# Sliding-window attention and a tanh-shrink layer on one core: batch 0's products with V by four query blocks, masks filled by VectorE, the first 760 steps in a new order

## The chip, the cores and the metric

The kernel runs on one core of one Trainium2 chip. A core has five engines that run side by side, each through its own list of instructions, in order: TensorE (PE, matrix products; PEld in the profile is its loading of weights), VectorE (DVE), ScalarE (ACT), GpSimd (POOL) and SyncE (SP). They wait for one another on semaphores. Data come from and go to the chip's memory by DMA transfers, which SP and POOL start here. Products land in PSUM, eight banks of 128 partitions x 2 KB; PE writes them, DVE and ACT read them, POOL does not.

The metric is the device time of one execution in microseconds (us).

## The reference

Eight batches of eight heads with 576 tokens of 64 numbers go through causal attention in a window of 64 tokens. The output, as 4,608 tokens of 512 numbers, goes through two dense layers.

```python
scores = scale * np.matmul(q, k.transpose(0, 1, 3, 2))
mask = (rel >= 0) & (rel < window)        # rel = query position - key position, window = 64
attn = softmax(where(mask, scores, -1e9))
x = matmul(attn, v), heads side by side   # 4608 x 512
h = x @ w_in                              # 512 x 2048
out = (h - np.tanh(h)) @ w_out            # 2048 x 512
```

## The kernel before

**Tiling.** A "group" g is a pair of heads of one batch (four groups to a batch, b = g // 4), and the 576 queries of a group are nine blocks of 64. A block of queries needs 128 keys. The tokens of all batches, put behind one another, are nine "chunks" of 512; a chunk c is worked through both dense layers by 16 tiles m of the hidden dimension and four row tiles s of the output. Since a batch has nine blocks and a chunk eight, the ninth block of batch 0 belongs to chunk 1.

**What sets the order.** Nothing is scheduled by a tool. A string PLAN lists some 2,000 steps, and `play` issues them one by one; each engine gets its instructions in the order in which the steps stand. A step is a short name with numbers, and ends in the engine's letter where it can run on several (p GpSimd, a ScalarE, v VectorE, s SP). A number at the end is often a PSUM bank. The steps that matter here, with the lines of the profile:

- `lk.g`, `lq.g` (L110): load K or Q of a group, 144 KB as stored; `LV.b.i`, `lv.b.pair.half` (L145, L132): load V; `wi.i` (L188), `wo.i` (L198): load parts of w_in (two of 256 columns, then three of 512) and w_out; `qr`, `lr`, `tq`, `tk`: rows of Q and K of batches 3 and later and their transposes by DMA on SP (L166, L171, L179).
- `U.n.bank` (L227): n products on a tile of zeros that nothing reads; fillers.
- `i` (L202), `h` (L230), `n` (L237): make the identity and two masks.
- `ck`, `cq` (L90 on ACT, L92 on DVE): cast or lay out rows for PE; `Fp`, `Ep` (L256, L260): PE's transposes of K and Q; `Fc`, `Ec` (L90, L92): copy them out of PSUM to kt and qp.
- `Rp.g.half.bank` (L281, L286): scores of five or four blocks; in batch 0 a product with the mask `hide` comes first. `Rx` (L318): Exp on ScalarE. `M` (L323): masking on VectorE, batch 1 and later.
- `zr`, `za`, `zb`, `Z`: copies of V between the halves of the partitions.
- `P`, `D`, `DS`, `DH` (L335, L375 to L390): in batch 0, a group's products with V into two banks, and the division by the row sums; `PP`, `DR`, `DN`: the same for two groups in later batches.
- `Xp`, `Xc` (L397): transposes of the attention output and their copies to x of a chunk (xT).
- `Hp.c.m.half`, `H.c.m` (L508, L431): first layer, a half or a whole tile m; `A` (L439): tanh; `G` (L445): the subtraction; `W.c.s.part` (L474): second layer; `O.c.s` (L90, L92 and a store by SP): output.

The products of the first layer of chunk 0 go round three PSUM banks, and of later chunks two; a bank is free when `G` has read it. GpSimd starts at most eight loads ahead: each further one waits until the load eight places before it has landed.

In batch 0, `P` did two banks of five blocks; as there are only nine, the ninth was computed twice:

```python
for n in range(2):
    for i in range(5):
        j = min(5 * n + i, NJ - 1)
```

Of the kernel before, what the change touches and what calls it, by code (L numbers as in the profile page):

```python
# [7 lines left out]
F32 = mybir.dt.float32  # L8
# [7 lines left out]
def kernel(  # L16
# [184 lines left out]
    def make_ident():  # L201
        nc.gpsimd.memset(ident, 0.0)  # L202
# [26 lines left out]
    def make_hide():  # L229
        nc.gpsimd.memset(hide, 0.0)  # L230
# [5 lines left out]
    def make_mask():  # L236
        nc.gpsimd.memset(seen, 1.0)  # L237
# [8 lines left out]
    def chunk_tile(c):  # L246
        return x_chunk[c % 3]
# [77 lines left out]
    def pv_banks(g):  # L325
        return ps[:, 0:2, :] if g == 2 else ps[:, 5:7, :]

    def pv(g):
        b, pr = divmod(g, NP)
        for n in range(2):  # L330
            for i in range(5):
                j = min(5 * n + i, NJ - 1)
                for h in range(2):
                    r = slice(64 * h, 64 * h + 64)
                    nc.tensor.matmul(pv_banks(g)[r, n, 65 * i:65 * i + 65], PT[g % NPT][:, j, r],  # L335
                                     vw[b % 2][:, j, pr + NP * h, :], start=True, stop=True)
# [34 lines left out]
    def norm(g):  # L371
        b, pr = divmod(g, NP)
        ov = pv_banks(g)[:, :, 0:5 * (D + 1)].rearrange("p n (i c) -> p n i c", c=D + 1)
        rc = sm_pool.tile([128, 2, 5, 1], F32, tag="rc", name="rc")
        nc.vector.reciprocal(rc, ov[:, :, :, D:D + 1])  # L375
        xo = xs[b % 2][:, pr // 2].rearrange("p (n i) r d -> p n i r d", i=5)
        nc.vector.tensor_tensor(xo[:, :, :, pr % 2, :], ov[:, :, :, 0:D], rc.to_broadcast([128, 2, 5, D]), ALU.mult)

    last = {}

    def norm_sums(g):
        ov = pv_banks(g)[:, :, 0:5 * (D + 1)].rearrange("p n (i c) -> p n i c", c=D + 1)
        last[g] = sm_pool.tile([128, 2, 5, 1], F32, tag="rc", name="rc")
        nc.vector.reciprocal(last[g], ov[:, :, :, D:D + 1])

    def norm_half(g, n):
        b, pr = divmod(g, NP)
        k = 5 - n
        ov = pv_banks(g)[:, n, 0:k * (D + 1)].rearrange("p (i c) -> p i c", c=D + 1)
        nc.vector.tensor_tensor(xs[b % 2][:, pr // 2, 5 * n:5 * n + k, pr % 2, :], ov[:, :, 0:D],  # L390
# [260 lines left out]
```

## Time and profile before

| | us |
|---|---|
| median of three runs | 307.96 (307.23 to 308.13) |
| span of the profiled execution | 305.2 |
| time around the span, median less span | 2.76 |
| PE busy | 297.8 (98%) |
| VectorE busy | 176.2 (58%) |
| ScalarE busy | 157.5 (52%) |
| GpSimd busy | 103.7 (34%) |

The profile shows one execution, from its first to its last instruction. The profiled execution's own time is known as its span alone, 305.2 us; the runs were timed apart from it. A line of the timeline reads: start in us, length in us, engine, source line, operation, output <- input, partitions x elements, how many were merged, and in brackets how long the engine was idle before and what ended that. A busy PE is not a PE at its peak: products overlap, and one with 512 columns is shown with 0.38 us while the next can start 0.21 us behind it.

### The profile page before, as it was taken

The page shows a single profiled execution, that of the slowest core. Times are in us where ns is not written, and L with a number is a line of the kernel's source. Part 1 is how long each engine was busy: PE and PEld are TensorE (multiplying, and loading weights), DVE is VectorE, ACT ScalarE, POOL GpSimd, SP SyncE. Part 2 cuts the span into 40 slices and gives each one's busy share as a digit, 9 for nine tenths or more (in the row PEclk, how much of TensorE's full clock was granted, in tenths as well). Part 3 has the DMA queues.
Part 4 walks back from the last instruction along what each step waited for, and adds up shares of the span by engine and source line. Part 5 has one row for each costly group of instructions (what it writes and reads, how often), then busy time and mean ns, then how long its engine had stood idle before and what let it go on. Part 6 is the DMA issues. An engine that isn't in the chain of part 4 may idle for free.

```text
span 305.2 us, 6469 instructions
## 1 busy us (share of the span) xinstructions
PE 297.8 (98%) x2599; PEld 149.4 (49%) x2632; DVE 176.2 (58%) x316; ACT 157.5 (52%) x265; POOL 103.7 (34%) x141
## 2 busy tenths in 40 slices
PE   8999999999999999999999999999999999999995
PEld 3574555545455545444544444444544444444443
DVE  1687993289577745675387475657673645355300
ACT  1898975487565346534564645345633433433211
POOL 8989775800994290019005770000000000000000
PEclk9999999999999999999999999999999999999999
DMA  9999999995999999949999999560143010001112
GB/s 155 159 195 193 195 207 180 159 205 102 102 143 127 173 125 181 182 108 131 164 177 127 135 173 142 95 143 35 37 76 74 0 69 37 34 34 37 52 51 104
DMA packets 132878, 36.77 MB, mean 120 GB/s; under 512 B 119920, under 2 KB 127344, under 8 KB 132848
## 3 DMA queue, kind: packets, MB, share of 16 engines
q0 software_dynamic: 92752, 18.06, 85.3%
q1 hardware_dynamic: 40096, 18.30, 31.5%
q8 instruction: 20, 0.33, 0.5%
q14 instruction: 10, 0.08, 0.1%
HBM read 36.70 MB, written 9.44 MB: 151 GB/s over the span
## 4 chain that ended last, share of the span: by engine, by line
PE 87%; DVE 5%; ACT 3%; issue 2%; POOL 2%; DVEq 0%; ACTq 0%; POOLq 0%
PE ps L474 38%; PE ps L431 30%; PE ps L508 6%; PE ps L348 3%; PE ps L304 2%; DVE gT L445 2%; PE ps L397 1%; ACT th L439 1%; PE ps L286 1%; PE ps L467 1%; DVE pt L323 1%; PE ps L260 1%; PE ps L281 1%; PE ps L227 1%; POOL qall L110 1%
## 5 line engine op out<-in xcount | busy, mean ns | idle before, releaser
L445 DVE TENSOR_TENSOR gT<-ps,th 128x512 bf16<-128x512 f32 x144 | 97.2, 687 | 85.3 <-ACT th L439 84.6
L474 PE MATMUL ps<-w_out_sb,gT 128*128 128x512 bf16 x527 | 131.5, 380 | 2.2 <-issue 0.8
L439 ACT ACTIVATE th<-ps 128x512 f32<-128x512 f32 x144 | 84.7, 599 | 93.0 <-PE ps L431 79.7
L431 PE MATMUL ps<-xT,wi 128*128 128x512 bf16 x496 | 120.7, 380 | 0.1
L474 PEld LDWEIGHTS <-gT 128*128 128x128 bf16 x560 | 53.3, 98 | 61.4
L431 PEld LDWEIGHTS <-wi 128*128 128x128 bf16 x496 | 47.0, 98 | 54.3
L145 POOL DMA_DIRECT2D vw<-in_v_dram x35 | 30.0, 872 | 36.1 <-PE ps L348 33.5
L90 ACT ACTIVATE ysb<-ps 128x512 f32<-128x512 f32 (+1 forms) x24 | 14.2, 593 | 30.9 <-PE ps L474 30.2
L166 POOL DMA_DIRECT2D qall<-in_q_dram x25 | 21.7, 881 | 24.1 <-DMA qw<-qall 21.4
L166 POOL DMA_DIRECT2D kall<-in_k_dram x25 | 21.7, 875 | 10.4 <-DMA kw<-kall 4.8
L314 ACT ACTIVATE pt<-ps 128x1024 bf16<-128x1024 f32 (+1 forms) x30 | 23.3, 816 | 3.5 <-PE ps L304 3.2
L323 DVE TENSOR_TENSOR pt<-pt,ps 128x1152 bf16<-128x1152 bf16 x28 | 20.5, 749 | 5.1 <-ACT pt L314 3.2
L508 PE MATMUL ps<-xT,wi 128*128 128x512 bf16 x80 | 20.8, 380 | 0.0
L92 DVE COPY ysb<-ps 128x512 f32<-128x512 f32 (+1 forms) x11 | 7.1, 650 | 20.5 <-PE ps L467 13.2
L368 DVE TENSOR_TENSOR xs<-ps,rcp 128x384 bf16<-128x384 f32 x28 | 15.2, 550 | 0.3
L318 ACT ACTIVATE pt<-ps 128x640 bf16<-128x640 f32 (+1 forms) x24 | 14.7, 659 | 0.8 <-PE ps L286 0.8
L348 PEld LDWEIGHTS <-pt 128*64 128x64 bf16 x504 | 9.4, 112 | 6.3 <-DVE pt L323 2.1
L90 ACT ACTIVATE kt<-ps 128x576 bf16<-128x576 bf16 x10 | 6.5, 647 | 10.8 <-PE ps L256 6.8
L227 PE MATMUL ps<-warm 128*128 128x512 bf16 (+1 forms) x35 | 10.6, 435 | 1.1 <-DVE warm L207 1.1
L508 PEld LDWEIGHTS <-wi 128*128 128x128 bf16 x80 | 7.4, 98 | 8.5 <-issue 0.4
L348 PE MATMUL ps<-vw,pt 128*64 128x65 bf16 x504 | 11.0, 197 | 0.3 <-DVE pt L323 0.2
L365 DVE TENSOR_TENSOR xs<-ps,rcp 128x384 bf16<-128x384 f32 x14 | 7.7, 550 | 0.1
(74 smaller groups left out, 166.7 us busy)
## 6 DMA issues: line engine op xcount, KB each, us to landing
out_dram<-ysb SPq DMA_DIRECT2D x33, 256.0 KB, 3.1
vw<-in_v_dram POOLq DMA_DIRECT2D x28, 128.0 KB, 6.6
qall<-in_q_dram POOLq DMA_DIRECT2D x20, 128.0 KB, 7.5
kall<-in_k_dram POOLq DMA_DIRECT2D x20, 128.0 KB, 6.8
w_out_sb<-in_moe_w_out_dram POOLq DMA_DIRECT2D x4, 512.0 KB, 8.2
kall<-in_k_dram POOLq DMA_DIRECT2D x11, 144.0 KB, 6.3
qall<-in_q_dram POOLq DMA_DIRECT2D x11, 144.0 KB, 6.6
wi<-in_moe_w_in_dram POOLq DMA_DIRECT2D x3, 512.0 KB, 7.9
```

Source lines behind the costliest of these rows:

```text
L90: nc.scalar.activation(o, i, ACT.Copy)
L145: nc.gpsimd.dma_start(out=w[:, 2 * i + 1, :, 0:D] if i < NF else w[64:128, 2 * i, :, 0:D], in_=v[b, :, 128 * i:128 * i + n].rearrange("h p ...
L166: nc.gpsimd.dma_start(out=token_rows(b, n)[0:c, i], in_=(q if n == "q" else k)[b, :, 128 * i:128 * i + c].rearrange("h p d -> p h d"))
L314: nc.scalar.activation(o, sp, ACT.Exp, scale=scale)
L323: nc.vector.tensor_tensor(p, p, mask.unsqueeze(1).to_broadcast([128, 2 * NJ, 64]), ALU.mult)
L348: nc.tensor.matmul(ps[r, bank, 65 * i:65 * i + 65], PT[(g + r2) % NPT][:, j, r], vw[b % 2][:, j, p0 + r2 + NP * h, :], start=True, stop=True)
L368: nc.vector.tensor_tensor(xs[b % 2][:, p0 // 2, 0:6, n // 2, :], ov[:, :, 0:D], sums[g][:, n].to_broadcast([128, 6, D]), ALU.mult)
L431: nc.tensor.matmul(hp, w_in_tile(ki, m), chunk_tile(c)[:, n.start // 64:n.stop // 64, ki % 2, 64 * (ki // 2):64 * (ki // 2) + 64], start=( ...
L439: nc.scalar.activation(th[:, n], hp, ACT.Tanh)
L445: nc.vector.tensor_tensor(gT[c][:, m, columns(s)], hp, th, ALU.subtract)
L474: nc.tensor.matmul(yp, gT[c][:, m, s * 128:(s + 1) * 128], w_out_sb[:, m, :], start=n == 1 and i == 0, stop=n == 4 and i == 3)
L508: nc.tensor.matmul(hp, w_in_tile(half + 2 * i, m), chunk_tile(c)[:, :, half, 64 * i:64 * i + 64], start=n == 1 and i == 0, stop=n == 2 and ...
```

## The change

In batch 0 the products with V of a group (`Pn`, `pv_part`) are made for four query blocks at a time, into one bank each (blocks 0 to 3 or 4 to 7), with their own reciprocals (`Dr`) and normalisation (`Dn`) on VectorE or, once, on ScalarE by four copies with a scale. The ninth blocks of all four groups are done together (`Pe`), normalised (`De`), transposed (`Xe`) and copied (`Xf`) to chunk 1. The transposes of xs in batch 0 then have four blocks in each part. A new step `iv` lets VectorE fill the identity's and the masks' tiles, which GpSimd did. The PLAN's steps up to `DR.22` stand in another order, with 16 fillers in place of 35; behind that step nothing is changed.

```diff
     def make_ident():
-        nc.gpsimd.memset(ident, 0.0)
         nc.gpsimd.affine_select(ident, ident, compare_op=ALU.not_equal, fill=1.0,
                                 base=0, pattern=[[-1, 128]], channel_multiplier=1)
+
+    def fill_masks():
+        nc.vector.memset(ident, 0.0)
+        nc.vector.memset(hide, 0.0)
+        nc.vector.memset(seen, 1.0)
...
-    def pv(g):
+    def pv_part(g, n, bank):
         b, pr = divmod(g, NP)
-        for n in range(2):
-            for i in range(5):
-                j = min(5 * n + i, NJ - 1)
-                for h in range(2):
-                    r = slice(64 * h, 64 * h + 64)
-                    nc.tensor.matmul(pv_banks(g)[r, n, 65 * i:65 * i + 65], PT[g % NPT][:, j, r],
-                                     vw[b % 2][:, j, pr + NP * h, :], start=True, stop=True)
+        for i in range(4):
+            j = 4 * n + i
+            for h in range(2):
+                r = slice(64 * h, 64 * h + 64)
+                nc.tensor.matmul(ps[r, bank, 65 * i:65 * i + 65], PT[g % NPT][:, j, r],
+                                 vw[b % 2][:, j, pr + NP * h, :], start=True, stop=True)
+
+    def pv_ends(b, bank):
+        for pr in range(NP):
+            for h in range(2):
+                r = slice(64 * h, 64 * h + 64)
+                nc.tensor.matmul(ps[r, bank, 65 * pr:65 * pr + 65], PT[(NP * b + pr) % NPT][:, NJ - 1, r],
+                                 vw[b % 2][:, NJ - 1, pr + NP * h, :], start=True, stop=True)
...
+    def norm_part(g, n, bank, eng):
         b, pr = divmod(g, NP)
...
+        if eng is nc.scalar:
+            for i in range(4):
+                nc.scalar.activation(xo[:, i], four(bank)[:, i, 0:D], ACT.Copy, scale=last[g, n][:, i])
+        else:
+            nc.vector.tensor_tensor(xo, four(bank)[:, :, 0:D], last[g, n].to_broadcast([128, 4, D]), ALU.mult)
...
     PLAN = """
-        u mv.0 mv.1 lk.1.p lq.2.p LV.0.2 U.1.3 U.1.3 U.1.5 U.1.7 U.1.6 lk.3.p U.1.1 U.1.7 lk.2.p U.1.7 lq.1.p
...
+        u iv U.8.3 U.4.4 lq.0.s lq.3.p lk.0.s i lk.2.p lk.3.p ck.0.a Fp.0.5 cq.0.a Fc.0.5.a mv.0 mt.0 mk mt.3
```

Three places show what moved. In the rows, kall0 and qall0 are the loaded K and Q of batch 0, kall1 and qall1 those of batch 1, vw0 is V of batch 0, ps the PSUM, pt the probabilities, xs the normalised attention output. The line numbers of the changed kernel are its own.

GpSimd's first transfers and masks, before:

```order
L110 DMA kall0_104<-in_k_dram 96x2x384
L110 DMA qall0_102<-in_q_dram 96x2x384
L145 DMA vw0_85<-in_v_dram 128x8x64
L110 DMA kall0_104<-in_k_dram 96x2x384 x2
L110 DMA qall0_102<-in_q_dram 96x2x384 x2
L145 DMA vw0_85<-in_v_dram 128x8x64
L202 MEMSET ident_75 128x128
L203 ISA
L203 AFFINE_SELECT ident_75<-ident_75 128x128
L145 DMA vw0_85<-in_v_dram 128x8x64 x2
```

and now:

```order
L110 DMA qall0_102<-in_q_dram 96x2x384
L202 ISA
L202 AFFINE_SELECT ident_75<-ident_75 128x128
L110 DMA kall0_104<-in_k_dram 96x2x384 x2
L145 DMA vw0_85<-in_v_dram 128x8x64
L110 DMA qall0_102<-in_q_dram 96x2x384
L110 DMA kall0_104<-in_k_dram 96x2x384
L234 AFFINE_SELECT hide_78<-hide_78 128x128
L236 AFFINE_SELECT hide_78<-hide_78 128x128
L145 DMA vw0_85<-in_v_dram 128x8x64 x3
L110 DMA qall0_102<-in_q_dram 96x2x384
L110 DMA kall1_105<-in_k_dram 96x2x384
```

The identity stands behind the first load in place of the eighth, both steps on `hide` come before the last V tiles, and the last Q of batch 0 (group 2's) is the tenth load, where it was the second.

ScalarE ahead of the copies to xT of chunk 0, before (from the eighth and last Exp of batch 0 to the first tanh):

```order
L318 ACTIVATE pt_87<-ps_74 128x640
L90 ACTIVATE kb2_111<-kall1_105 96x2x6x64
L90 ACTIVATE kt0_88<-ps_74 128x576
L90 ACTIVATE qp0_94<-ps_74 128x576
L90 ACTIVATE qb2_108<-qall1_103 96x2x6x64
L90 ACTIVATE kt1_89<-ps_74 128x576
L318 ACTIVATE pt_87<-ps_74 128x512
L90 ACTIVATE xT0_112<-ps_74 128x4x128
L90 ACTIVATE kb1_110<-kall1_105 96x2x6x64
L439 ACTIVATE th_596<-ps_74 128x512
```

and now, from the copy of group 2's Q on:

```order
L90 ACTIVATE qp2_96<-ps_74 128x576
L320 ACTIVATE pt_87<-ps_74 128x512
L390 ACTIVATE xs0_115<-ps_74,rh_404 128x64 x4
L320 ACTIVATE pt_87<-ps_74 128x640
L320 ACTIVATE pt_87<-ps_74 128x512
L90 ACTIVATE qb1_107<-qall1_103 96x2x6x64
L90 ACTIVATE kt2_90<-ps_74 128x576
L90 ACTIVATE xT0_112<-ps_74 128x4x128
L90 ACTIVATE qb0_106<-qall1_103 96x2x6x64
L90 ACTIVATE xT0_112<-ps_74 128x4x128 x2
```

Two casts of batch 1's Q (qb) stand between the last Exp of batch 0 and the copies to xT, and ScalarE does one normalisation in four parts.

VectorE from the V copies to the first normalisation, before:

```order
L92 COPY vw0_85<-vw0_85 64x520 x6
L92 COPY kb1_110<-kall1_105 96x2x6x64
L375 RECIPROCAL rc_386<-ps_74 128x10
L377 TENSOR_TENSOR xs0_115<-ps_74,rc_386 128x10x64
L92 COPY qb1_107<-qall1_103 96x2x6x64
```

and now:

```order
L92 COPY vw0_85<-vw0_85 64x520 x8
L92 COPY kb0_109<-kall1_105 96x2x6x64
L383 RECIPROCAL rh_400<-ps_74 128x4
L383 RECIPROCAL rh_402<-ps_74 128x4
L383 RECIPROCAL rh_404<-ps_74 128x4
L392 TENSOR_TENSOR xs0_115<-ps_74,rh_402 128x4x64
L392 TENSOR_TENSOR xs0_115<-ps_74,rh_400 128x4x64
```

The cast kb0 (step `ck.6`, K of group 6, the eleventh load) stands ahead of three reciprocals in a row, and each normalisation covers four blocks of one group in place of ten.

More of the change, by code (lines that the diff above doesn't have):

```diff
@@ L379 @@
[L379 to L390, printed above, removed]
-                                last[g][:, n, 0:k].to_broadcast([128, k, D]), ALU.mult)
+    last = {}
@@ new lines, in norm_ends, with x_ends @@
+    def norm_ends(b, bank):
+        rc = sm_pool.tile([128, 4, 1], F32, tag="rh", name="rh")
+        nc.vector.reciprocal(rc, four(bank)[:, :, D:D + 1])
+        for half in range(2):
+            n = slice(2 * half, 2 * half + 2)
+            nc.vector.tensor_tensor(xs[b % 2][:, half, NJ - 1], four(bank)[:, n, 0:D],
+                                    rc[:, n].to_broadcast([128, 2, D]), ALU.mult)
+    def x_ends(b, bank):
+        tp = ps[:, bank, :].bitcast(BF16)[:, 0:256].rearrange("p (r t) -> p r t", t=128)
+        for half in range(2):
+            nc.tensor.transpose(tp[:, half, :], xs[b % 2][:, half, NJ - 1].rearrange("p r d -> p (r d)"), ident)
@@ L400, in x_put @@
     def x_put(b, half, part, bank, eng):
-        w0, w1 = 4 * part, 4 + 5 * part
+        w0, w1 = 4 * part, 4 + (5 if b else 4) * part
         tp = ps[:, bank, :].bitcast(BF16)[:, 0:640].rearrange("p (w t) -> p w t", t=128)
```

190 lines of the change are left out of this document (95 added, 95 removed).

## The prediction

> **What bounds the kernel now.** I read the page's busy times first, then the chain that ended last, then what TensorE (PE) waited for.
>
> ```profile
> PE 297.8 (98%) x2599; PEld 149.4 (49%) x2632; DVE 176.2 (58%) x316; ACT 157.5 (52%) x265; POOL 103.7 (34%) x141
> PE 87%; DVE 5%; ACT 3%; issue 2%; POOL 2%; DVEq 0%; ACTq 0%; POOLq 0%
> PE ps L227 <- DVE warm L207: 1.1, 1, 1.1
> PE ps L474 <- issue: 0.8, 5, 0.2
> ```
>
> PE carries 87% of the chain and hardly waits: its longest wait for another engine is the first 1.1 us. Nothing that only frees ScalarE, VectorE or GpSimd can shorten this kernel. What can go is work of PE that computes nothing: the filler products of line 227.
>
> ```profile
> L227 PE MATMUL ps<-warm 128*128 128x512 bf16 (+1 forms) x35 | 10.6, 435 | 1.1 <-DVE warm L207 1.1
> 1.06 6.54 PE L227 MATMUL ps<-warm 128*128 128x512 bf16 x22 [1.06 <-DVE warm L207]
> 8.33 1.90 PE L227 MATMUL ps<-warm 128*128 128x512 bf16 x7
> 1.47 0.15 PEld L227 LDWEIGHTS <-warm 128*128 128x128 bf16 x1 [0.28 <-issue]
> 1.89 0.15 PEld L227 LDWEIGHTS <-warm 128*128 128x128 bf16 x1 [0.28 <-issue]
> 4.56 2.55 PEld L227 LDWEIGHTS <-warm 128*128 128x128 bf16 x12 [0.28 <-issue]
> 22.58 1.54 PE L508 MATMUL ps<-xT,wi 128*128 128x512 bf16 x6
> ```
>
> Fillers of 512 columns start 0.43 us apart at first (1.47 to 1.89) and about 0.21 apart from 4.56 on (12 in 2.55), so PE runs at half pace for its first 3.5 us. All 35 take about 6.5 + 1.7 + 6 x 0.22 = 9.5 us of PE's time. They cover the time in which the inputs arrive and attention of batch 0 is too short of work; the first product with w_in (step Hp.0.0.0) starts at 22.58. From there PE is dense, as the stages show:
>
> ```profile
> 5.50:22.58 17.08, 16.63 (x324) 10.64 (x323) 10.84 (x30) 13.14 (x22) 15.15 (x26) 1.00 1.70 176
> 22.58:41.12 18.54, 18.52 (x207) 9.48 (x205) 16.01 (x34) 16.48 (x31) 14.17 (x23) 1.00 1.44 196
> 41.12:195.00 153.88, 152.11 (x1402) 77.05 (x1423) 97.92 (x168) 85.41 (x144) 70.06 (x85) 1.00 1.79 149
> ```
>
> (Columns: stretch, its length, busy PE, weight loads, DVE, ACT, POOL, clock, DMA, GB/s.) After 41 us there is nothing to win, only something to lose. So the question is when Hp.0.0.0 starts in the new order, and whether PE stays fed behind it.
>
> **The change part by part.** *Fillers.* 19 of 35 go. Twelve stand at the start: 8 at 0.43 and 4 at 0.21 from 1.06 end at about 5.3; four more (0.86 us) stand before the third group of scores. That is 5.1 us in place of 9.5. The 4.4 us are saved only if PE has real work then; else they become waits.
>
> *Work before and behind Hp.0.0.0.* These rows give prices on PE:
>
> ```profile
> 18.98 0.43 PE L260 MATMUL ps<-ident,kb 96*128 96x96 bf16 x6
> 14.11 0.29 PE L286 MATMUL ps<-qp,kt 64*128 64x64 bf16 x8
> 16.06 0.51 PE L335 MATMUL ps<-vw,pt 128*64 128x65 bf16 x20
> ```
>
> By Hp.0.0.0 the new order has done less: one transposed half of batch 1 in place of four (3 x 0.25, without the 0.17 tail of the last), no Rp.4.1.5 (0.3), 16 fewer products with V (0.35) and 2 fewer transposes of xs (0.1): 1.5 us. Of that 8 products (0.18) are gone for good, the last blocks no longer being done twice, and two later fillers (0.43) go too. So 0.9 us more is left behind Hp.0.0.0, and the change breaks even if that step starts at 22.58 - 0.9 = 21.7.
>
> *When it can start: the loads.*
>
> ```profile
> 1.28 0.43 SPq L110 DMA_DIRECT2D qf<-in_q_dram  x1
> qf<-in_q_dram SPq DMA_DIRECT2D x1, 288.0 KB, 3.7
> 7.53 0.48 PEld L256 LDWEIGHTS <-qall 96*64 96x64 bf16 x12 [0.42 <-DMA qall<-in_q_dram]
> 15.30 0.65 POOL L110 DMA_DIRECT2D qall<-in_q_dram  x1 [0.27 <-DMA vw<-in_v_dram]
> 21.04 0.64 POOL L110 DMA_DIRECT2D qall<-in_q_dram  x1 [0.83 <-DMA wi<-in_moe_w_in_dram]
> ```
>
> SP's second load lands at 1.28 + 3.7 = 5.0; it is K of group 0 now, and ScalarE's cast can begin then, where before it began at 9.11. GpSimd's loads share some 176 GB/s. Before, its second had landed by 7.5, its tenth by 15.3 (GpSimd, eight loads on, waits for it), its seventeenth (10 x 144 + 4 x 128 + 64 + 2 x 256 = 2,528 KB in) by 21.0. In the new order its tenth load is Q of group 2, the last input that batch 0's attention needs; the first ten carry the same 6 x 144 + 4 x 128 KB. I take 14.6, between 13.5 (no queueing behind it) and 15.3.
>
> *When it can start: the engines.* Durations:
>
> ```profile
> 9.11 0.84 ACT L90 ACTIVATE kb<-kf 96x768 bf16<-96x768 f32 x1
> 11.46 0.65 ACT L90 ACTIVATE qp<-ps 128x576 bf16<-128x576 bf16 x1
> 13.37 3.50 ACT L318 ACTIVATE pt<-ps 128x640 bf16<-128x640 f32 x6
> 22.26 0.60 ACT L90 ACTIVATE xT<-ps 128x512 bf16<-128x512 bf16 x1
> 44.88 0.77 ACT L90 ACTIVATE xT<-ps 128x384 bf16<-128x384 bf16 x2 [0.79 <-PE ps L397]
> 15.76 0.36 DVE L92 COPY kb<-kall 96x768 bf16<-96x768 bf16 x1
> 16.68 0.22 DVE L375 RECIPROCAL rc<-ps 128x10 f32<-128x10 f32 x1 [0.56 <-PE ps L335]
> 21.14 0.41 DVE L390 TENSOR_TENSOR xs<-ps,rc 128x256 bf16<-128x256 f32 x1
> ```
>
> Back to back, ScalarE's jobs start about 0.1 sooner than their durations say (six Exp in 3.50). Group 0's scores can begin near 8.7, when the third load has been transposed, four us earlier than before. But PE then outruns the loads: from Q of group 2 at 14.6 on there are its transposes (to 15.0), the copy on ScalarE (15.1 to 15.7) and one Exp (to 16.2). VectorE meanwhile stands in step ck.6, whose K of group 6 is the eleventh load (15.5), and only then does its three reciprocals (0.22 each); behind it stand all normalisations, so the banks of PE too. ScalarE resumes at about 16.9 with the four scaled copies of Dn.3.1.6. No row shows a copy of 128x64: 0.07 each by elements from the 128x384 copies (0.77 for two), 0.39 if as long as one of those; I take 0.2, nearer the small end. Then in its order two Exp, the cast cq.4, a copy, an xT copy, the cast cq.6 and the last xT copy: 0.8 + 1.1 + 0.73 + 0.53 + 0.48 + 0.73 + 0.6 = 5.0. Hp.0.0.0 starts at 21.8 or so; with the ends of both unknowns, 20.4 to 22.9. Against 21.7 that is a loss of 0.1 us. The two casts (1.5 us) belong to batch 1 and stand ahead of a copy on which PE waits.
>
> *The first layer behind it.*
>
> ```profile
> 27.79 2.75 PE L431 MATMUL ps<-xT,wi 128*128 128x512 bf16 x12
> 29.55 1.63 ACT L439 ACTIVATE th<-ps 128x512 f32<-128x512 f32 x3
> ```
>
> PE needs 0.86 us a tile; sixteen tanh at about 0.5, with the casts, copies and Exp between, are about 15 of the 16.5 us that PE takes here, so ScalarE just keeps up. The weights come in the order wi.0, wi.3, wi.1, wi.2, wi.4. wi.3 is complete at 2,928 KB: (2,928 - 2,528) / 196 behind 21.0 is 23.0, likewise wi.1 24.4, wi.2 27.0, wi.4 30.3. Counting its work from Hp.0.0.0 on, PE wants them at about 24.8, 27.4, 28.7 and 32, so each has 1.7 us to spare. The three banks of the first layer are freed tile by tile (tanh, then VectorE's subtraction): I find two waits of 0.2 there, so I charge 0.4 us, between 0 and 1.2.
>
> *Batch 1's products with V, behind the W steps.* They now wait at the end of VectorE's two maskings and two V copies (0.7 each), which start once the Exp of group 7 is done, behind an output copy on ScalarE. I get 51.2 against PE's 50.7: 0.4, ends 0 and 1.
>
> *Masks.* Three fills move from GpSimd to VectorE:
>
> ```profile
> 7.02 0.27 POOL L202 MEMSET ident<- 128x128 bf16 x1
> 8.18 0.76 DVE L92 COPY qp<-ps 128x576 bf16<-128x576 bf16 x1 [5.21 <-PE ps L256]
> ```
>
> They fall into VectorE's 5.2 us of idle time: nothing; were it busy, 0.1 each. On GpSimd they free 0.3 us each, and its loads wait for their turn on the DMA engines anyway. *Casts moved to GpSimd* (ck.4, cq.9, cq.10, ck.11): about 0.9 us each by elements (768 for 520) from the row below. K of group 4 is there near 28 and PE asks for it at 31.6; for cq.10 I get 57.4 against 61. So nothing; if that cover fails, 0.9 each on PE, and the loads queued behind them are as late.
>
> ```profile
> 29.43 0.61 POOL L92 COPY vw<-vw 64x520 bf16<-64x520 bf16 x1
> ```
>
> *Switches between kinds of products on PE*: scores of batch 1 now stand singly in places, two more returns to long products, 0.1 each: 0.2.
>
> The sum: 305.2 + 0.1 + 0.4 + 0.4 + 0.2 = 306.3 us of span. The median of 307.96 is 2.76 more than the profiled span, which I keep: 309.1.
>
> **The rivals.** *Faster: the ladder is shorter.* It decides from Hp.0.0.0 before 20.6, so that 1.1 us is gained and what follows costs nothing. If Q of group 2 lands at 13.5, PE's own chain of scores (to about 14) governs, ck.6 does not wait, and with short scaled copies Hp.0.0.0 starts near 20.4: 307.96 - 1.3 = 306.7. For it speaks that ScalarE works from 5.0, not 8.4; against it the tenth load at 15.3 in the row above.
>
> *Slower: PE falls back to half pace.* From 5.3 to about 8.7 PE has 36 short transposes, some 1.2 us of work in 3.4, where before fillers filled such gaps. If it then runs at half pace until it has been busy as long as at the start, some 5 us of real work up to 16 (six sets of scores at 0.5 with their masks, five transposed halves at 0.3) take twice as long, half of that in waits that are there anyway: +2.5, 311.6. The granted clock reads 1.00 in each stretch, even where the first fillers run at half pace, so it cannot exclude it. [...]
>
> *Slower: a late V copy.*
>
> ```profile
> 75.95 5.94 POOL L145 DMA_DIRECT2D vw<-in_v_dram  x7 [15.41 <-PE ps L348]
> 71.37 24.11 SPq L171 DMA_TRANSPOSE kw<-kall  x3
> vw<-in_v_dram POOLq DMA_DIRECT2D x28, 128.0 KB, 6.6
> ```
>
> GpSimd's queue already stands 15 us behind PE once. In the new order loads of batch 5 (qr.5.1), which need batch 3's transposes on SP done, stand ahead of LV.3.0, which VectorE's Z.3 needs at about 85. Batch 1's last products free V's buffer near 56; some twenty issues at 0.85 (seven in 5.94) and a wait for SP bring GpSimd to LV.3.0 near 76, and it lands 6.6 later, near 83. Four us later still it would hold VectorE for 2, and PE through the banks: +2, 311.
>
> **How the numbers follow.** No change is told from a change of under 0.3%, 0.92 us. The forecast has 0.55 (0.33 of it slower by more, 0.22 within 0.92 us, by the ends of its four terms, 307.5 to 310.5), the short ladder 0.26, half pace 0.07, the late V copy 0.12. So faster 0.26, same 0.22, slower 0.52. The range leaves out 0.1 on each side: 306.5 to 311.4.
>
> **What would show it.** Right: Hp.0.0.0 (first product on xT) between 21 and 22.5; VectorE idle before ck.6's copy until K lands; ScalarE without a gap from 17 to 21.5; PE's waits up to there some 5 us in place of fillers; first-layer tiles done near 39. Wrong: Hp.0.0.0 before 20.6; any product of 512 columns 0.43 apart behind 5.3; a PE wait of over 1 us behind 41.

## The result and the profile after

The changed kernel takes 312.29 us (median of four, 310.68 to 312.74), the kernel before 307.94 on the same chip: a ratio of 1.0137 (95% interval 1.0106 to 1.0168), 4.35 us slower. The forecast had the sign right (309.1, slower with 0.52), but the time lies above its range, which ended at 311.4. The ratios here and below leave out the executions over 1.5% longer than the fastest of the same kernel (four, all with two or four stretches at half pace: two with five output buffers, one with Q of group 2 earlier, one with six fillers); the medians don't.

The page of the changed kernel, its busy times, the clock that PE was granted (in 40 slices of 7.8 us, tenths of full speed) and the chain that ended last:

```profile
PE 299.2 (96%) x2571; PEld 150.0 (48%) x2605; DVE 177.3 (57%) x325; ACT 158.2 (51%) x268; POOL 105.4 (34%) x141
PEclk9957999999999999999999999999999999999999
PE 90%; DMA 4%; POOL 2%; issue 1%; DVE 1%; ACT 1%; POOLq 0%; DVEq 0%; ACTq 0%
```

The third and fourth slices are new: PE runs there at half pace in part. And PE now waits, where before it had one wait of 1.1 us at the start and little else:

```profile
PE ps L526 <- DMA xT<-xs: 1.8, 1, 1.8
PE ps L258 <- DMA qall<-in_q_dram: 1.2, 2, 0.8
PE ps L231 <- DVE warm L211: 1.1, 1, 1.1
PE ps L415 <- DVE xs L392: 1.0, 2, 0.7
PE ps L333 <- ACT pt L320: 0.7, 1, 0.7
```

The stages of the changed kernel, cut where the granted clock changes (columns as in the prediction; the clock is the third number from the end):

```profile
10.08:13.49 3.41, 3.41 (x62) 1.82 (x60) 1.80 (x6) 2.79 (x5) 3.41 (x6) 1.00 1.76 157
13.49:16.90 3.41, 1.90 (x62) 1.40 (x56) 1.22 (x6) 1.97 (x4) 3.15 (x5) 1.00 1.29 172
16.90:20.31 3.41, 3.41 (x54) 2.17 (x53) 2.48 (x11) 2.90 (x8) 2.76 (x6) 0.50 1.40 193
20.31:23.73 3.42, 2.40 (x25) 1.80 (x24) 1.21 (x4) 3.42 (x6) 1.58 (x3) 0.50 1.33 203
23.73:27.14 3.41, 3.41 (x19) 1.71 (x16) 0.70 (x3) 1.85 (x4) 1.50 (x3) 0.50 1.26 205
```

From 16.90 to 27.14 us the clock is 0.50. That is 10.24 us, three stretches of 3.41: in two other profiles (below) the clock stays at 0.50 for 3.41 us, and full pace lasts 10.24 us here ahead of the fall (from 6.66), 283.31 behind it (83 stretches) and 300.37 in the profile before (4.70 to 305.07, 88 stretches). In the stretch ahead of the fall PE was busy for 1.90 of 3.41 us.

The rows of PE on the ladder that the prediction built, and the one late wait:

```profile
14.39 0.45 PE L258 MATMUL ps<-ident,qall 96*64 96x96 bf16 x12 [0.82 <-DMA qall<-in_q_dram]
16.08 0.70 PE L333 MATMUL ps<-vw,pt 128*64 128x65 bf16 x32 [0.69 <-ACT pt L320]
23.57 1.06 PE L526 MATMUL ps<-xT,wi 128*128 128x512 bf16 x2
149.51 0.59 PE L526 MATMUL ps<-xT,wi 128*128 128x512 bf16 x2 [1.84 <-DMA xT<-xs]
```

L526 is the first half product of a chunk, and its first row is Hp.0.0.0: at 23.57, where before it stood at 22.58. The second of its two products starts at 23.99, 0.43 behind the first: half pace. The last row is Hp.4.0.1, which waits for a transpose of xs by DMA (step Y.4.1, L434). SP issued that transpose behind two transposes of K and a store:

```profile
139.31 2.51 SPq L171 DMA_TRANSPOSE kw<-kall  x2
141.91 0.53 SPq L513 DMA_DIRECT2D out_dram<-ysb  x1
142.54 3.06 SPq L434 DMA_TRANSPOSE xT<-xs  x2
```

Before, the same step left 6.4 us earlier (3.8 earlier than in the second profile of the changed kernel, below), and no PE wait of over 0.2 us stood in the second half of the kernel:

```profile
136.13 2.62 SPq L416 DMA_TRANSPOSE xT<-xs  x2
```

ScalarE's four scaled copies, whose price no row of before showed:

```profile
17.23 0.93 ACT L390 ACTIVATE xs<-ps,rh 128x64 bf16<-128x64 f32 x4 [1.20 <-DVE rh L383]
```

So there were two suspects, the half pace and the wait of 1.84 us.

### The profile page after: what moved, and what is told of

The parts are those of the page before. It is cut to its first block, busy times and chain, and to the rows that moved or that the text cites. A ratio compares the mean times of both kernels' runs of the same rounds, so it can differ in the third digit from the quotient of the medians.

```text
span 310.9 us, 6430 instructions
## 1 busy us (share of the span) xinstructions
PE 299.2 (96%) x2571; PEld 150.0 (48%) x2605; DVE 177.3 (57%) x325; ACT 158.2 (51%) x268; POOL 105.4 (34%) x141
## 4 chain that ended last, share of the span: by engine, by line
PE 90%; DMA 4%; POOL 2%; issue 1%; DVE 1%; ACT 1%; POOLq 0%; DVEq 0%; ACTq 0%
PE ps L492 38%; PE ps L449 34%; PE ps L526 6%; PE ps L353 3%; DMA xT<-xs 2%; PE ps L306 2%; DMA qall<-in_q_dram 2%; PE ps L415 2%; PE ps L262 2%; PE ps L288 1%; PE ps L485 1%; POOL vw L145 1%; PE ps L333 1%; POOL kall L110 1%; POOL qall L110 0%
## 5 line engine op out<-in xcount | busy, mean ns | idle before, releaser
L492 PE MATMUL ps<-w_out_sb,gT 128*128 128x512 bf16 x526 | 129.9, 379 | 2.0 <-issue 0.5
L325 DVE TENSOR_TENSOR pt<-pt,ps 128x1152 bf16<-128x1152 bf16 x28 | 20.4, 750 | 8.4 <-ACT pt L316 4.7
L526 PE MATMUL ps<-xT,wi 128*128 128x512 bf16 x80 | 22.4, 398 | 2.0 <-DMA xT<-xs 1.8
L166 POOL DMA_DIRECT2D qall<-in_q_dram x25 | 21.5, 863 | 4.0 <-DMA qw<-qall 2.0
L320 ACT ACTIVATE pt<-ps 128x512 bf16<-128x512 f32 (+1 forms) x24 | 15.0, 652 | 8.2 <-PE ps L288 7.4
L373 DVE TENSOR_TENSOR xs<-ps,rcp 128x384 bf16<-128x384 f32 x28 | 14.8, 550 | 0.2
L92 POOL COPY q<-qw 64x256 bf16<-64x256 bf16 x3 | 1.2, 402 | 34.6 <-DMA qw<-qall 34.6
L526 PEld LDWEIGHTS <-wi 128*128 128x128 bf16 x80 | 7.7, 102 | 9.9 <-issue 2.9
L90 ACT ACTIVATE xT<-ps 128x512 bf16<-128x512 bf16 (+3 forms) x12 | 5.8, 516 | 6.4 <-PE ps L415 6.4
L110 POOL DMA_DIRECT2D qall<-in_q_dram x11 | 7.3, 670 | 3.2 <-DMA w_out_sb<-in_moe_w_out_dram 1.9
```

Source lines behind the costliest of these rows:

```text
L90: nc.scalar.activation(o, i, ACT.Copy)
L166: nc.gpsimd.dma_start(out=token_rows(b, n)[0:c, i], in_=(q if n == "q" else k)[b, :, 128 * i:128 * i + c].rearrange("h p d -> p h d"))
L320: nc.scalar.activation(PT[g % NPT][:, js[0]:js[0] + len(js), :].rearrange("p i (h t) -> p i h t", h=2), sp, ACT.Exp, scale=scale)
L325: nc.vector.tensor_tensor(p, p, mask.unsqueeze(1).to_broadcast([128, 2 * NJ, 64]), ALU.mult)
L492: nc.tensor.matmul(yp, gT[c][:, m, s * 128:(s + 1) * 128], w_out_sb[:, m, :], start=n == 1 and i == 0, stop=n == 4 and i == 3)
L526: nc.tensor.matmul(hp, w_in_tile(half + 2 * i, m), chunk_tile(c)[:, :, half, 64 * i:64 * i + 64], start=n == 1 and i == 0, stop=n == 2 and ...
```

## The experiments

All ran beside the kernel before: the run without its last six fillers on one chip (median of the kernel before 308.06), all others on another, called the second chip below (307.70 to 307.95). A useful measure comes with each execution: its mean granted clock. One stretch of 3.41 us at half pace lowers the mean over some 309 us by 3.41 x 0.5 / 309 = 0.0055, so a clock of 0.994 means one such stretch, 0.989 two and 0.983 three. The values of 0.997 to 0.999 I put down to the very end of a run, behind its last products: in the profile of the new code in the old order (0.998) the last 1.4 us are at half pace, in the first of the changed kernel the last 0.42, and PE does nothing there.

### The changed kernel again

No edit.

> The changed kernel once more, unaltered, on the same chip as the experiments beside it, for its spread and its granted clock from execution to execution. If the fall of the clock is what makes its executions differ, those of clock 1.00 are some 2 us shorter than those near 0.985. Rival (the landing of transfers makes them differ): executions of equal clock differ by as much.

311.11 us (309.12 to 313.47, ten executions), ratio 1.0095 (1.0061 to 1.0129). Three executions had a clock of 0.998 or more: 309.12, 309.66 and 309.94, mean 309.57. The other seven had 0.993 to 0.995, one stretch at half pace each: 310.77 to 313.47, mean 311.81. The first chip's four fit: 310.68 at 1.00, 312.02 and 312.74 at 0.989 and 0.988, 312.57 at 0.983. The kernel before never fell below 0.998 in the 88 executions beside these runs. Over both chips the four executions at full pace have a mean of 309.85, the ten with half pace 312.00, 2.1 us more. Executions of equal clock still differ by up to 2.7 us, so the rival has a part too.

The profiled one had a clock of 1.00 and a span of 308.0. Its waits and its Hp.0.0.0:

```profile
PE ps L258 <- DMA qall<-in_q_dram: 1.4, 2, 0.8
PE ps L526 <- DMA xT<-xs: 1.3, 1, 1.3
PE ps L415 <- DVE xs L392: 1.2, 2, 0.7
PE ps L231 <- DVE warm L211: 1.1, 1, 1.1
PE ps L262 <- ACT kb L90: 0.8, 1, 0.8
PE ps L449 <- DVE gT L463: 0.7, 1, 0.7
PE ps L333 <- ACT pt L320: 0.7, 1, 0.7
...
22.22 0.59 PE L526 MATMUL ps<-xT,wi 128*128 128x512 bf16 x2
```

At full pace Hp.0.0.0 starts at 22.22. With three more waits of 0.3, 0.2 and 0.2 PE waits 6.8 us behind its start, against 0.4 before; 2.0 of the 6.8 (xT and gT) lie behind 41 us.

What the half pace itself costs is seen when the two profiles of this one kernel are laid side by side. ScalarE's scaled copies start at 17.23 in the first, where half pace has just begun (16.90 to 27.14), and here at 17.20; the first Exp behind the half pace starts there at 28.64 and here at 25.55:

```profile
17.20 0.93 ACT L390 ACTIVATE xs<-ps,rh 128x64 bf16<-128x64 f32 x4 [1.20 <-DVE rh L383]
28.64 0.60 ACT L320 ACTIVATE pt<-ps 128x512 bf16<-128x512 f32 x1 [1.19 <-PE ps L288]
25.55 0.60 ACT L320 ACTIVATE pt<-ps 128x512 bf16<-128x512 f32 x1 [0.44 <-ACT th L457]
```

(The middle row is of the first profile, the others of this one.) So the two are level to 0.03 us up to the fall, and the first is 3.1 us late behind three slow stretches, though PE waited no longer in it (1.2 us between 17 and 41, against 1.7 here). At the end it is 2.9 us late, the whole difference of the two spans. In one stretch at half pace PE can lose no more than half of it, 1.7 us. The seven executions with one stretch are 2.2 us longer in the mean than the three without, so the half pace is most of that but, as far as so few can tell, not all: a load that lands late makes PE wait, and the same wait empties a stretch (in the first profile the 0.82 us on Q of group 2 lie in the stretch from 13.49, ahead of the fall).

### The kernel before without 13 fillers

```diff
-Fp.1.5 U.1.2 Ec.2.3.v ... mt.1 U.1.1 U.1.3 U.1.2 U.1.4 mt.2 U.1.1 U.1.4 cq.0.a ... Ep.1.3 U.1.7 Fp.3.5
+Fp.1.5 Ec.2.3.v ... mt.1 mt.2 cq.0.a ... Ep.1.3 Fp.3.5
...
-P.3 U.1.3 lk.6.p ... lq.7.p U.1.4 ... Rp.4.1.5 U.1.1 ... Hp.0.1.0 U.1.5 ... N U.1.7
+P.3 lk.6.p ... lq.7.p ... Rp.4.1.5 ... Hp.0.1.0 ... N
```

> The kernel before without its 13 fillers behind the first 22 (3.2 us of PE's time between 8 and 28 us). Theory of the clock: without them PE has waits there, the granted clock falls under 1.00 somewhere between 12 and 27 us, and the time rises by 1 to 3 us, to 309 to 311. Rival 1 (the fillers cost what they take): 305.0. Rival 2 (waits take their place and the clock stays at 1.00): 307.6 to 308.

308.57 us, ratio 1.0031 (1.0007 to 1.0054). Nine of ten executions had a clock of 0.983 to 0.994, and the time goes with it: 307.82 at 1.00; 308.03 in the mean with one stretch (five), 309.15 with two (three), 310.02 with three (one). The clock fell where the theory said, but the rise in time is below its 1 to 3 us. Neither rival came: some 3 us less work of PE made the kernel slower by 0.8 in the medians (0.2 to 1.7 by the ratio). The stretches of the profile, cut at the same period:

```profile
5.63:9.05 3.42, 3.06 (x35) 1.44 (x33) 0.57 (x1) 0.32 (x1) 3.35 (x6) 1.00 1.54 176
9.05:12.46 3.41, 2.05 (x60) 1.70 (x60) 1.50 (x7) 3.22 (x6) 3.27 (x8) 1.00 2.16 163
12.46:15.87 3.41, 3.16 (x36) 1.34 (x36) 2.66 (x9) 2.51 (x5) 2.86 (x5) 0.50 1.81 153
15.87:19.28 3.41, 3.41 (x54) 1.78 (x52) 0.53 (x3) 2.36 (x4) 2.89 (x5) 0.50 1.40 193
```

Again the clock falls behind a stretch in which PE was busy for little more than half: 2.05 of 3.41 us. No PE wait in it was over 1.6 us.

### The kernel before without its last six fillers

```diff
-Ep.1.3 U.1.7 Fp.3.5 ... P.3 U.1.3 ... lq.7.p U.1.4 ... Rp.4.1.5 U.1.1 ... Hp.0.1.0 U.1.5 ... N U.1.7
+Ep.1.3 Fp.3.5 ... P.3 ... lq.7.p ... Rp.4.1.5 ... Hp.0.1.0 ... N
```

> The kernel before without its last 6 fillers (1.3 us of PE's time, between 11 and 28 us), while the 7 near 8 to 10 us stay. Theory (the clock falls only behind a stretch of 3.4 us in which PE is busy for less than about 0.6; in the run without all 13 that was 9.0 to 12.5 us, and every other stretch was at 0.9): the clock is 1.00 in all executions, and the time is 0 to 0.8 us below the kernel before, since some 0.5 us of the 1.3 come back as waits. Rival (any wait in these first 30 us may bring the half pace): clocks of 0.994 and 0.989 appear, as in the run without 13, and the time is 0.3 to 0.9 us above the kernel before.

307.60 us (306.23 to 308.20), ratio 0.9974 (0.9959 to 0.9989): this beats both kernels, the one before by 0.3 to 1.3 us. All twelve executions had 0.998 or more. The lowest stretch of its first 27 us:

```profile
10.23:13.65 3.42, 3.07 (x67) 2.06 (x64) 1.56 (x7) 3.20 (x6) 3.28 (x8) 1.00 2.50 138
```

3.07 of 3.42 us busy, and no fall. This kernel and the one without 13 differ only in the seven fillers near 8 to 10 us: with them, which take 1.5 us, its median is 1.0 us lower, and 1.3 when each is taken against the kernel before on its own chip. In the profiles, ScalarE's cast of K behind the first Exp starts at 21.05 without the seven (half pace from 12.46 to 19.28) and at 19.23 with them, though at 9 us the run without them was 0.6 ahead. Here the half pace is shown as a cause, by an edit.

So it isn't any wait that brings the half pace. Over all 14 profiles (both kernels and the twelve runs) I laid stretches of 3.41 us, on the grid that each one's clock shows: 97 at full pace begin in the first 30 us. In five PE was busy for 1.58 to 2.05 us, and each of the five was followed by half pace; in the other 92 it was busy for 2.19 us or more, and none was. The run with five output buffers has the lowest one:

```profile
13.09:16.50 3.41, 1.58 (x34) 0.91 (x34) 1.71 (x6) 2.00 (x5) 1.90 (x4) 1.00 1.28 176
16.50:30.16 13.66, 12.11 (x142) 7.67 (x141) 5.91 (x21) 8.96 (x17) 9.20 (x15) 0.50 1.32 200
```

But over the whole run busy time alone does not part the stretches. Later in the same traces PE is busy as little and the clock stays, so around the late wait in the first profile of the changed kernel:

```profile
146.61:150.02 3.41, 1.57 (x8) 0.67 (x7) 0.33 (x1) 0.99 (x2) 2.14 (x3) 1.00 1.80 111
150.02:153.44 3.42, 3.42 (x18) 1.53 (x17) 2.06 (x4) 1.91 (x4) 0.00 (x0) 1.00 2.73 150
```

There all products are large, in the first 30 us most are small. Let a product of 128x128 weights with 512 columns, such as a filler, count as one unit, and each other one by its share of that: a transpose with 96x64 weights and 96 columns as 0.07. A product is spread over the time that its columns take, 0.21 us for 512 at full pace and 0.43 at half. At full pace 16 such units fit into a stretch (3.41 / 0.21). By this count, an estimate of mine worked out from the shapes and times of the traces' products, the five stretches ahead of a fall hold 3.7 (from 13.09 with five output buffers) to 5.2 units (from 13.49 in the changed kernel), and the one from 146.61 holds 6.5. Over the whole of the 14 traces, at full pace every stretch with 5.2 units or less was followed by half pace (these five, and those at the ends of the runs, behind the last products), none with 5.8 or more was, and none lies between. Half pace went on behind stretches of up to 5.9 units and ended behind those with 6.0 or more. I read this count off the traces after the runs; no run was made to test it.

### Fillers back in the changed kernel

```diff
-Fp.3.7 ... Ep.1.4 ... Ep.2.3 ... Pn.3.1.6 ... Xp.0.1.1.5 ... Xp.0.1.0.1
+U.1.4 Fp.3.7 ... U.1.0 Ep.1.4 ... U.3.2 Ep.2.3 ... U.2.0 Pn.3.1.6 ... U.1.7 Xp.0.1.1.5 ... U.3.7 Xp.0.1.0.1
```

> The changed kernel with 13 filler products put back, at six places of its first 23 us at which PE waits anyway (two by two in front of waiting transposes, scores and products with V). Theory of the clock (PE, kept half busy by waits, is granted half pace from 16 to 27 us): the granted clock is 1.00 in every stretch and every run, products on xT behind 23 us are 0.21 apart, and the time is about 1.9 us below the 312.3 of the changed kernel, near 310.4. Rival (the clock is only a symptom of the waits, or the 1.9 us are something else): fillers take PE's time or nothing, 312.3 to 313.

These are eleven products, not thirteen as the expectation says, here and below. 312.28 us (309.61 to 312.56, four executions), ratio 1.0130 (1.0074 to 1.0186). Two had a clock of 1.00 (309.61 and 312.56), two 0.993 and 0.995. The theory missed: half pace still came in two of four, and the median is the rival's.

### One transpose and one tile moved

```diff
-tq.5.4 tk.6.3 tk.5.0 ... Y.4.1 ... Hp.4.0.0 ... A.3.13 ... G.3.13 ... W.3.0.3
+tq.5.4 tk.5.0 ... Y.4.1 tk.6.3 ... A.3.13 G.3.13 W.3.0.3 Hp.4.0.0
```

> The changed kernel with two things moved near 140 us: one DMA transpose of K of group 6 of a later batch (tk.6.3) goes behind the transpose of xs for chunk 4 (Y.4.1) on SP, and one tile's tanh, subtraction and part of the second layer (A.3.13, G.3.13, W.3.0.3) go ahead of Hp.4.0.0. Theory (PE's wait of 1.84 us on that transpose at 147 is a loss in full): the wait is gone and the time is 1.8 us lower, about 310.5. Rival (the wait is given back later, since the rest of the queue is as late): about 312.3, with a wait of the same size at a later transpose.

310.79 us (309.53 to 312.77, seven executions), ratio 1.0102 (1.0067 to 1.0138). The profiled one had one stretch at half pace. The wait on xT is gone; of PE's waits behind 41 us the profile lists

```profile
PE ps L492 <- ACT ysb L90: 0.8, 1, 0.8
PE ps L449 <- DVE gT L463: 0.5, 1, 0.5
```

ScalarE waited for 1.17 us, until 128.97, for a store to land and free a row buffer (ysb), and PE behind it. Beside the changed kernel on this chip (311.11) the gain is 0.3 us, not 1.8, and within the noise. The rival is nearer: the wait was given back at other places, though not at a later transpose.

### Five output buffers

The edit just shown, with another buffer count:

```diff
+    y_pool = ctx.enter_context(tc.tile_pool(name="y", bufs=5))
-        ysb = sm_pool.tile([128, d_model], F32, tag="ysb", name="ysb")
+        ysb = y_pool.tile([128, d_model], F32, tag="ysb", name="ysb")
```

> The changed kernel with the transpose and the tile moved as in the second experiment, and five buffers in place of three for the output rows on their way to memory, so that ScalarE needn't wait near 128 us until a store has landed. No filler is added. Theory (the wait on the transpose was a full loss, and in the second experiment a wait on a store took 0.8 us of its place): PE has no wait over 0.6 us behind 41 us, and the time is 1.5 us below the changed kernel on this chip, about 309.6, and near 308.3 in executions of clock 1.00. Rival (PE's waits in the back only move): 310.8 as before, with other waits of the same sum.

310.91 us (308.29 to 313.64), ratio 1.0087 (1.0060 to 1.0114). The profile (clock 0.978, four stretches at half pace) has one PE wait behind 41 us, gT with 0.5. At full pace its three executions had 308.29 to 309.88, mean 309.15, against 309.57 of the unaltered one; the five with two stretches had 311.35, against 312.38 for the first chip's two. So the cures of the back may bring something between 0.4 and 1.0, not the 1.5 expected; with three executions a side it can't be settled closer. Laid beside the profile of the changed kernel at full pace, this one makes up 0.8 us between 147 and 160 us, where the other waits 1.3 us on xT.

### Both cures, and a shorter way to Hp.0.0.0

The edits of the two runs called first and second experiment here, fillers back and one transpose and one tile moved, together:

> The changed kernel with both the 13 fillers of the first experiment and the new place of the DMA transpose and of one tile of the second. Theory (two losses, the clock's 1.9 us and the 1.8 us of the wait on the transpose, which add up): 3 to 3.7 us below the changed kernel on the same chip, about 308.6 to 309.3. Rival (each gain is spent by waits that come up behind it): within 1.5 us of the changed kernel.

310.80 us (309.53 to 311.86), ratio 1.0072 (1.0042 to 1.0102). All seven executions had 0.999 or more: the half pace is gone. The time isn't what the sum promised, only 0.3 below the unaltered one, as the rival had it. The profile (span 308.2) lists three waits of PE over 0.4 us:

```profile
PE ps L258 <- DMA qall<-in_q_dram: 1.6, 2, 1.4
PE ps L231 <- DVE warm L211: 1.1, 1, 1.1
PE ps L449 <- DVE gT L463: 0.5, 1, 0.5
```

Behind the start PE waits 3.6 us in all, 3.2 less than at full pace without the cures; but the eleven fillers take 11 x 0.22 = 2.4 themselves. At equal clock these seven, with a mean of 310.61, are 1.0 us longer than the three of the unaltered kernel (309.57). So in the changed kernel the half pace can be bought off, and that costs about what it saves.

```diff
-Pn.3.1.6 Pn.0.0.5 Pn.1.0.2 Pn.0.1.3 ... Pn.2.1.4 ... cq.6.a ... Dn.2.1.4.v ... Pn.2.0.1 Dr.2.0.1 Dn.2.0.1.v ... Xc.0.0.0.2.a
+Pn.1.0.2 Pn.0.1.3 Pn.3.1.6 Pn.0.0.5 ... Pn.2.1.4 Pn.2.0.1 ... Dn.2.1.4.v Dr.2.0.1 Dn.2.0.1.v ... Xc.0.0.0.2.a cq.6.a
```

> As the run with both, and the way to Hp.0.0.0 shortened: the products with V that use banks 2 and 3 ahead of those in banks 5 and 6, the last such products of group 2 and their division ahead of the transposes of xs, the cast of Q of group 6 behind a copy to xT, and two of the 13 fillers left out. Theory (what is left of the loss is that PE waits ahead of Hp.0.0.0): it starts 0.6 to 0.9 us earlier than in the first experiment, near 21.6, and the time is 0.6 to 0.9 below the run with both, so 307.7 to 308.7. Rival (ScalarE or VectorE gives it back in the first layer): no difference to the run with both.

Four of the eleven fillers are left out here. 310.72 us (308.44 to 311.79), ratio 1.0069 (1.0037 to 1.0101); nothing between it and the run with both can be told, so the rival holds. Hp.0.0.0 started at 22.09 in its profile, against 22.36 in the first experiment and 23.54 in the run with both.

### Q of group 2 earlier

```diff
-LV.0.3 LV.0.2 LV.0.0 lq.2.p
+lq.2.p LV.0.3 LV.0.2 LV.0.0
```

> As the run with five output buffers, and Q of group 2 (the tenth load, on which the prediction's ladder stood) three places earlier in GpSimd's queue, ahead of three loads of V. Theory (this load sets when Hp.0.0.0 starts): it lands near 12, PE's wait ahead of its transposes is gone, Hp.0.0.0 starts 0.5 to 1 us earlier, and the time is as much lower. Rival (the V loads, now later, and K of group 6 set it): no difference, with the wait ahead of the first product with V longer by what the other is shorter.

310.58 us (308.55 to 313.20), ratio 1.0085 (1.0054 to 1.0115), against 1.0087 with five buffers: no difference. The rows of PE:

```profile
13.85 0.45 PE L259 MATMUL ps<-ident,qall 96*64 96x96 bf16 x12
15.75 1.02 PE L334 MATMUL ps<-vw,pt 128*64 128x65 bf16 x32 [0.91 <-ACT pt L321]
22.41 1.06 PE L527 MATMUL ps<-xT,wi 128*128 128x512 bf16 x2
```

(This kernel's lines stand one lower in its text, so its L527 is L526 of the changed kernel.) The transposes of Q no longer wait, the first products with V wait longer, and Hp.0.0.0 stands where it stood. The rival holds: the load was not the rung that sets the ladder. This profile, too, prices the half pace: from 17.4 to 22.0 us it is level with that of the changed kernel at full pace to 0.05 us, and behind its one slow stretch, 22.04 to 25.45, it is 1.7 us late.

### Six fillers at two places

```diff
-ck.4.p Ep.2.3 ... ck.6.v Pn.3.1.6
+ck.4.p U.3.2 Ep.2.3 ... ck.6.v U.3.0 Pn.3.1.6
```

> As the run with five output buffers, and six fillers at the two places where PE waits in every trace of the changed kernel so far (three ahead of the transposes of Q of group 2, three ahead of the first products with V). Theory (the fall of the clock comes from the stretch of 13 to 17 us, where PE is busy for little more than half, and costs about 1.5 us in most executions): the clock is 1.00 in nearly all executions and the time 1 to 1.5 us below the run with five buffers, about 308.5. Rival (PE's half pace is hidden by waits that are there anyway): the clock is 1.00 and the time the same as of the run with five buffers, within 0.5.

309.97 us (308.15 to 313.52), ratio 1.0064 (1.0040 to 1.0089). Both theory and rival had the clock wrong, and the 0.9 us below the run with five buffers in the medians is less than the ratios (1.0064 and 1.0087) can tell. Only five of eleven executions were at full pace, so the low stretch isn't always the one at 13 to 17 us: in the run with Q of group 2 earlier it was 18.62 to 22.04, in the one with the transpose moved 7.36 to 10.77. Where the grid of 3.41 us lies differs from execution to execution: full pace began at 3.94 in the profile of the run with the transpose moved, at 4.70 in that of the kernel before and at 6.82 in that of the kernel before without its last six fillers. The two stretches, of the run with Q of group 2 earlier

```profile
18.62:22.04 3.42, 1.96 (x35) 1.49 (x35) 1.97 (x7) 3.42 (x8) 3.38 (x6) 1.00 1.27 184
```

and of the one with the transpose moved:

```profile
7.36:10.77 3.41, 1.91 (x47) 1.39 (x48) 2.06 (x6) 1.65 (x3) 3.41 (x6) 1.00 1.72 156
```

### The new code in the old order

The parts of the change put into the old PLAN, with its 35 fillers:

```diff
-... P.3 U.1.3 ... D.3 ... Xp.0.1.0.7 ... Xc.0.1.1.1.v Rx.4.1.5 ... N U.1.7
+... Pn.3.0.5 Pn.3.1.6 Pe.0.7 U.1.3 ... Dr.3.0.5 Dr.3.1.6 Dn.3.0.5.v Dn.3.1.6.v ... Xp.0.1.0.7 ... De.0.7 Rx.4.1.5 ... N Xe.0.3 Xf.0.3.v U.1.7
```

> The changed kernel's code (products with V by four query blocks, the ninth blocks together, masks filled by VectorE) in the order of the steps and with the 35 fillers of the kernel before. Theory (all of the loss comes from the new order of the steps): 307.9, within 0.6. Rival (more, smaller instructions on VectorE and the extra banks cost in themselves): 309 to 311.

309.41 us (308.61 to 309.93), ratio 1.0050 (1.0030 to 1.0070). But in bank 7 the transpose of xs overwrites the ninth blocks of batch 0 before they are divided, so the ninth blocks of batch 0 are made from the overwritten values, and PE waits for the late copy:

```profile
PE ps L526 <- ACT xT L90: 1.1, 1, 1.1
```

With the transpose in bank 4:

> The run of the new code in the old order, with one bank changed: there the ninth blocks of batch 0 shared bank 7 with a transpose of xs, PE waited 1.1 us for ScalarE at the second half of the first products on xT, and the values in the bank were overwritten; now the transpose uses bank 4. Theory (the code costs nothing, the loss of that run was this collision): within 0.6 us of the kernel before, about 308. Rival (the code itself costs, whatever the bank): 309.0 to 309.5 again, with a wait in the first 30 us that is not this one.

308.51 us (308.11 to 309.29), ratio 1.0008 (0.9989 to 1.0027), and PE's longest waits behind the start are

```profile
PE ps L333 <- ACT pt L320: 0.4, 1, 0.4
PE ps L262 <- DVE xT L92: 0.3, 1, 0.3
```

So the code by itself, masks on VectorE included, costs nothing that can be told, and at most 0.8 us by the interval. The loss is that of the new order with its 16 fillers.

## Why the prediction was wrong

*The step that failed: the half pace as a rival at 0.07.* The mechanism stood in the prediction, with its price: 2.5 us. Half pace came in ten of 14 executions, and those took 2.1 us longer than the other four; in the two profiles laid side by side it cost 3.1 us for three stretches. So the price was near, though worked out for another place (up to 16 us), and the chance was wrong: what was left out of the sum at 0.07 was the usual case. Three readings went into it. The first place was argued too narrowly: only 5.3 to 8.7 us was thought of, where in the first profile the low stretch was 13.49 to 16.90, with 1.90 of 3.41 us busy. The second: the granted clock was held unable to show a half pace, since it reads 1.00 over the slow first fillers. In the profiles it does show each fall to 0.50, and only the start, ahead of the first grant (to 4.70 us in the profile before, while fillers stood 0.43 apart), is filled in with 1.00. The third: saved fillers were counted against waits of PE one for one, while a wait also empties a stretch, which a filler, one full unit in 0.21 us by the count above, doesn't. That half pace would last until PE had been busy as long as at the start was an estimate from the start alone; the falls in five profiles lasted 3.41 to 13.65 us. Of the three signs named for a wrong forecast two came: products of 512 columns 0.43 apart behind 5.3 us, and a PE wait of over 1 us behind 41.

The clock fell behind stretches without any gap over 1.7 us (PE's longest wait there was 1.67 in the run with five output buffers, up to 1.6 in the kernel before without 13 fillers, 0.82 in the first profile of the changed kernel), with PE busy for 0.46 to 0.60 of the time (1.58 to 2.05 of 3.41 us) in mostly small products.

*Fillers.* Held in part. In the profile at full pace the twelve at the start were done at 5.1 us, and the 16 together took 4.9 us instead of the forecast's 5.1; in the first profile all twelve stood 0.43 apart, and the last started at 5.73.

*The ladder to Hp.0.0.0.* The rungs came as forecast: Q of group 2 at 14.39 (14.6 forecast), the first four scaled copies of ScalarE at 17.23 (16.9), at 0.93 for the four in place of 0.8; and at full pace Hp.0.0.0 at 22.22, against 21.8 within 20.4 to 22.9. In the first profile of the changed kernel it was 23.57, in the one with four slow stretches 25.07, and in the full-pace profiles with fillers put back 22.09 to 23.64. But the rung named as first, the load, did not carry it: with it earlier, the first products with V came at 15.75 in place of 16.05, and nothing behind them came earlier, so the start came out right though the load that was to set it did not set it: that part is luck. At full pace this part about breaks even, as forecast: PE waits 4.8 us ahead of 41 us, and 4.6 us of fillers are gone (9.5 less 4.9).

*"After 41 us there is nothing to win, only something to lose."* Right, and the loss was looked for at one place alone, the V copy at about 85. No PE wait stood there, so that rival is out. The loss came on SP's queue instead: Y.4.1 6.4 us later and 1.8 us of wait in one profile, 3.8 and 1.3 in another. SP's transposes up to DR.22 were part of the new order, and of the late ones none was walked through. Its effect on the time is smaller than its wait, 0.4 to 1.0, since stores and gT held PE next.

*The first layer and batch 1's products with V.* 0.4 each were charged. The one profile at full pace has 0.2 of gT ahead of 41, and 0.7 behind; on V it waited 0.2 or 0.3 in three other profiles, less than the 0.4. Both terms were somewhat high.

*The sum.* Without half pace 309.1 was forecast; the four executions of the changed kernel at full pace on both chips have 309.12 to 310.68, mean 309.85. So the sum was short by some 0.75, about what Y.4.1 costs. The profile at full pace is 2.8 us longer than that before: waits 6.4 more, fillers 4.6 less, and 1.0 that no view gives to a cause, as waits under 0.2 us aren't listed. The times differ by less than those profiles, 309.85 against 307.94: the timed executions of the kernel before have spans of 304.8 to 307.9, mean 306.2, and the profiled one had 305.2. Of the 2.76 us that the sum adds, some 0.9 is only that the profiled execution was a short one; each timed one is 1.7 to 2.0 longer than its span.

*Masks, casts, switches.* Costed at nothing or 0.2. The new code in the old order agrees for the masks (in the changed kernel VectorE's three fills took 0.11, 0.11 and 0.17 us). No run shows the switches by themselves; in the trace before a first long product starts 0.12 us behind the last of a set of scores, and a first score 0.31 behind a long product, where the next long one starts 0.22 behind.

What stays open: why executions of equal clock differ by 2 to 3 us (the kernel before does too, 306.6 to 309.7). In one profile PE waited 1.48 us for a transpose at a place that neither the change nor an experiment touches, behind the step DR.22:

```profile
180.04 1.46 PE L527 MATMUL ps<-xT,wi 128*128 128x512 bf16 x6 [1.48 <-DMA xT<-xs]
```

That points to how transfers land, but was not tested.

## What to carry to other kernels

When fillers or dense work are taken from PE, look not at the longest gap but at the work that PE gets in every stretch of some 3.4 us, wherever the grid lies (here full pace began between 3.9 and 6.8 us), and count products by their size: in the 14 traces here half pace followed each stretch with 5.2 full products or less out of 16 and none with 5.8 or more, while the busy share misled, with falls at 0.60 and none at 0.46. The executions of the changed kernel with half pace took about 2 us longer. Fillers are worth their time where a stretch would else fall under that, and cost their time elsewhere: the kernel before needs the seven near 8 to 10 us of its 13 late ones, and is some 0.5 us faster without the other six. When an order is written anew, walk every queue to its end, the DMA transposes of SP too; what is late there shows up 100 us behind the place one is looking at.

## What was unexpected in the hardware

- The granted clock falls without any long gap (1.67 us at most): behind 3.41 us with PE busy for 1.58, 1.90, 1.91, 1.96 and 2.05 us. One stretch with 2.19 us busy was not followed by a fall, nor were later ones of large products alone with 1.57 and 1.98.
- A fall lasts one stretch or several: 3.41 us in two profiles, 6.83, 10.24 and 13.65 in three. It ended behind a stretch with PE busy throughout in all five, but one such stretch (16.90 to 20.31 in the changed kernel) did not end it: by the count above it held 5.6 units, those five 6.0 to 7.8.
- The grid differs from execution to execution: in the 14 profiles full pace was first granted between 3.9 and 6.8 us, though each kernel started its first product at 1.06. So the same 22 fillers at the start took 6.54 us in the profile where it came at 4.70 and 7.59 where it came at 6.82.
